# TensorE adds the denominator's two terms in the last five groups of a fused FFT and two-layer MoE kernel

## The chip, the cores and the metric

The kernel runs on one core of one Trainium2 chip. The metric is the device time of one execution in microseconds. Three executions of the kernel before took 1020.41, 1020.96 and 1021.34 us; the median is 1020.96 us.

## The reference

`x` (2 x 3008 x 256, f32) goes through a Fourier transform along the sequence and then along the features, and the real part is kept. The 6016 tokens of 256 features then pass through two dense layers with 2048 hidden units each:

```python
x = fft(fft(x, axis=1), axis=2).real            # 6016 x 256
h = x @ w1_in;  x = (max(h, 0) ** 2) @ w1_out   # first layer
h = x @ w2_in                                   # second layer
P = a[0] + a[1]*h + a[2]*h**2 + a[3]*h**3
Q = 1 + abs(b[0])*abs(h) + abs(b[1])*h**2
out = (P / (Q + 1e-6)) @ w2_out
```

All inputs and outputs are f32.

## The kernel before, in words

Tokens are columns, features and hidden units are partitions. The first layer works on 12 tiles of tokens (one of 384, eleven of 512); the second on 23 sub-tiles, numbered t = 0 to 22: one of 384 tokens and 22 of 256. A sub-tile's 2048 hidden units are 16 chunks of 128. A *group* (t, j) of the second layer is two chunks of 256 tokens side by side, one PSUM bank of 128x512; the last sub-tile, t = 22, has seven such groups (j = 0 to 6) and two single chunks of 128x256 (j = 7 and 8).

Big products are made in parts: each operand is a high and a low part of type F32R, so a chunk costs 3 x 2 matmuls into the hidden layer (line 770) and 3 x 2 out of it (line 824). An F32R matmul is one instruction in the trace. A matmul whose operands are plain F32 is two instructions with two weight loads: the 20 calls of `q_mm` (line 667) have 40 instructions. Both print as f32.

A group of the second layer takes these steps; the letters are the names of the operations in the code:

- `h2` (TensorE, line 770): H2 = W_in x, 12 matmuls of 256 columns for a wide group, 6 for a single.
- `u` (ScalarE, line 890): u = |s h| into SBUF; `t1` (ScalarE, line 904): a3 h + a2.
- `t2`, `t3` (VectorE, lines 920 and 925): Horner's steps for P without a0; both read H2.
- the denominator without its 1, in one of two ways. In most groups `q` (VectorE, line 910) writes (u + b0) h over H2 in the PSUM bank, and `w` (ScalarE, line 916) takes its absolute value in place. In the groups of the list `SUMS`, `v` (ScalarE, line 895) squares a scaled h into SBUF and `w` (GpSimd, line 899) adds it to u. `q` comes after `t3`, since it overwrites H2.
- `y`, `z` (ScalarE, lines 931 and 935): reciprocal square root of the denominator (1 is the bias), then its square, so z = 1/Q. In the groups of the list `ALONE`, `P` (ScalarE, line 939) adds a0 to the polynomial.
- `gh` (VectorE, line 947, or GpSimd, line 946, in `ALONE` groups), `m`, `e` (VectorE, lines 953 and 958 or 962), `c2` (GpSimd, in the last two groups VectorE, line 967): g = P/Q as a high part and a low part that makes up for the rounding.
- `o2` (TensorE, line 824): 12 matmuls (6 for a single) that add the group into the output bank o2a. Of each six, the two with the low part of g come last.

After the 16 chunks of a sub-tile, `oa` (ScalarE, line 984) copies o2a to SBUF, a DMA (line 985) writes it out, and the bank is free for the next sub-tile's first `o2`.

`SUMS` holds the groups of t <= 2 and, in the last two sub-tiles, those with j % 4 == 1. So of the last five groups (22,4) to (22,8), before the change (22,5) is in `SUMS`, (22,4) and (22,6) are in `ALONE`, and (22,7) and (22,8) are the last two (`FIN`).

Every engine executes its instructions in the order of a table: `ORDER` (line 60 on) holds, for each engine, two-digit numbers in base 62, each the place of an operation among those added for that engine. `TIES` holds pairs in which an instruction of GpSimd is made to wait for one of VectorE. `Queues.run` merges the five tables into one program and gives out buffers by an estimate of times; the `cost` given to `add` is such an estimate and has no part in the result. An engine that waits for one instruction's inputs executes nothing that stands behind it in its table.

Of the kernel before, what the change touches and what calls it, by code (L numbers as in the profile page):

```python
# [9 lines left out]
F32 = mybir.dt.float32  # L10
# [39 lines left out]
def f32(ap):  # L50
# [22 lines left out]
    "4w50GWGX4t4x4u4v4yGb4zGdGcGRGi54Ge51GfGS521u53EKGg58GhGk1v55Gn56Gj5759Gp5A5C5BGlGoGmGsGqGu5DGx5GGrGt"
    "5E5FGyGvH2GwGz5H5KH45IH35JH0H1H95OHAH55L5M5P5S5N5QH65RHBHEHF5WHCHD5T5UHJHK5V1wHOHPHG5aHH5X5Y1xHI5ZH7"
    "HLH85bHTHUHM5eHNHQ5cHR5d5i5f5gHSHYHZHV5hHdHW5mHX5jHe5k5lHiHaHjHbHc5n5qHpHf5oHg5p5r5uHqHhHkHl5s5y5tHr"
    "HmHs5vHt5wHuHv5zHzI05x606261HwI4HxI5Hy66I1631y64I265HnI3I66A67I9HoIA68I71z69ELI86EIEIF6BIJIBIKIC6CID"
    "IGIH6D6FIIIO6G6I6HILIMIN6MIP6J6Q6K6LIVIWIaIb6NIQIfIRISIg6R6OIXIY6P6U6SIZ6TIhIcIdIeIkIlIpIqIiIj6V6WIT"
    "6YIUIuImIv6XInIo6Z6cIr6g6a6bIs206dIt6e6fIzIwJ0J4J56hIx6kIy6iJ16jJ26oJ36l6m6n6sJBJC21J6J76p6qJ8JGJH6r"
    "JDJEJF6tJL6w6u70JM6v6xJIJJ6yJKJQ716zJN74JOJR7273J9JV78JWJPJS75JAJT76EMJU79777C7AJaJb7BJXJYJfJg7GJZJc"
    "7KJd7DJe7E7F7H7IJkJlJrJsJh7JJiJj227LJm7M7NJn7OJo7SJtJuJv7P7QJw7RJx7TK17UK2K6K7Jy7VJzK0237WJpK3K4K57X"  # L80
    "7a7YJq7ZKBKC7b7eK87cK9KA7dKDKGKHKLKM7i7fKEKF7gKQKIKJ7hKKKR7mKN7j7kKO7l24KP7nKX257qKYKS7oKT7p7rKU7sKc"
    "7u7tKdKZ7yKaKbKhKi7vKe7wKm7xKnKf827zKgKj8081KkKVKlKrKsKo8384KW86Kp85KwKxKqKtKuKv878826ENL1L2898AL6Ky"
    "Kz8EL08B8CL7L38DL48IL527L8L9LA8FLDLE8G8J8H8KLI8LLJ8MLFLNLOLG8QLHLK8NLL8OLM8P8R8SLB8T8ULP8YLSLTLQLCLR"
    "8VLXLY8W8c8Z8X8aLc8bLULdLV8gLWLZLa28Lb8k8d8eLhLi8h8f8i29Le8jLfLgLjLk8oLlLm8lLn8m8nLtLu8pLyLz8sM3LoM4"
# [1126 lines left out]
```

## Time and profile before

| | |
|---|---|
| median of three executions | 1020.96 us |
| the profiled execution's own time | 1020.44 us |
| its span, first to last instruction | 1018.70 us |
| TensorE busy | 1000.1 us |
| VectorE busy | 977.9 us |
| ScalarE busy | 950.4 us |
| GpSimd busy | 637.3 us |

The profiled execution's time is 1.74 us more than its span: what lies around the first and the last instruction. "Busy" of TensorE counts pipelined matmuls, each printed with its latency (0.28 us for 256 columns) and not with the spacing of a stream (some 0.11 us), so starts, not durations, tell its pace. The clock granted to TensorE is shown as a share of 2.4 GHz.

### The profile page before, as it was taken

The page shows a single profiled execution, that of the slowest core. Times are in us where ns is not written, and L with a number is a line of the kernel's source. Part 1 is how long each engine was busy: PE and PEld are TensorE (multiplying, and loading weights), DVE is VectorE, ACT ScalarE, POOL GpSimd, SP SyncE. Part 2 cuts the span into 40 slices and gives each one's busy share as a digit, 9 for nine tenths or more (in the row PEclk, how much of TensorE's full clock was granted, in tenths as well). Part 3 has the DMA queues.
Part 4 walks back from the last instruction along what each step waited for, and adds up shares of the span by engine and source line. Part 5 has one row for each costly group of instructions (what it writes and reads, how often), then busy time and mean ns, then how long its engine had stood idle before and what let it go on. Part 6 is the DMA issues. An engine that isn't in the chain of part 4 may idle for free.

```text
span 1018.7 us, 20462 instructions
## 1 busy us (share of the span) xinstructions
PE 1000.1 (98%) x7378; PEld 946.5 (93%) x7378; DVE 977.9 (96%) x1766; ACT 950.4 (93%) x1918; POOL 637.3 (63%) x562
## 2 busy tenths in 40 slices
PE   9999999999999999999999999999999999999997
PEld 9989988999999999999999999999999999999986
DVE  5999999898999999999999999999999999999998
ACT  3789998999999999999999999999999999999996
POOL 0000068899866766767676676866766677767486
PEclk9999999999999999999999999999999999999999
DMA  9665500000000000001000001000000000000000
GB/s 346 215 209 160 156 1 1 16 1 27 23 1 17 1 22 12 12 4 30 11 12 11 12 2 32 1 12 22 1 12 26 7 11 12 1 12 9 3 12 22
DMA packets 19701, 38.12 MB, mean 37 GB/s; under 512 B 2078, under 2 KB 12208, under 8 KB 19600
## 3 DMA queue, kind: packets, MB, share of 16 engines
q1 hardware_dynamic: 19487, 36.42, 10.5%
q8 instruction: 58, 0.95, 0.4%
q10 hardware_dynamic: 112, 0.39, 0.1%
q14 instruction: 44, 0.35, 0.1%
HBM read 27.99 MB, written 8.81 MB: 36 GB/s over the span
## 4 chain that ended last, share of the span: by engine, by line
PE 80%; DVE 12%; ACT 3%; DMA 2%; issue 2%; POOL 1%; POOLq 0%; SPq 0%; DVEq 0%; ACTq 0%
PE o2a L824 22%; PE p L770 18%; PE o1a L824 11%; PE o1b L824 11%; PE p L800 9%; PE o2b L770 4%; PE o2b L800 2%; DMA xt<-in_dram 1%; DVE cw L480 1%; DVE g L947 1%; DVE cw L485 1%; DVE t L920 1%; DMA x2l<-in_dram 1%; DVE g L873 1%; PE p L783 1%
## 5 line engine op out<-in xcount | busy, mean ns | idle before, releaser
L824 PE MATMUL o2a<-g,w2hi 128*128 128x256 f32 (+1 forms) x1440 | 256.4, 282 | 4.4 <-POOL g L967 4.0
L873 POOL TENSOR_TENSOR g<-g,g 128x512 fp32r<-128x512 f32 x160 | 208.2, 1304 | 81.6 <-ACT g L867 40.2
L967 POOL TENSOR_TENSOR g<-t,y 128x512 fp32r<-128x512 f32 x150 | 203.2, 1360 | 42.0 <-DVE t L962 20.7
L824 PEld LDWEIGHTS o2a<-g,w2hi 128*128 128x128 f32 x1440 | 207.6, 189 | 9.6 <-POOL g L967 5.5
L848 POOL TENSOR_TENSOR g<-g,bc 128x256 f32<-128x256 f32 x160 | 127.0, 795 | 98.8 <-DVE g L845 39.0
L824 PE MATMUL o2a<-g,w2lo 128*128 128x256 f32 (+1 forms) x720 | 144.2, 280 | 0.0
L824 PE MATMUL o1b<-g,w1hi 128*128 128x512 f32 x352 | 138.3, 393 | 0.0
L824 PE MATMUL o1a<-g,w1hi 128*128 128x512 f32 x352 | 138.2, 393 | 0.0
L899 POOL TENSOR_TENSOR u<-u,y 128x512 f32<-128x512 f32 (+1 forms) x34 | 42.1, 1243 | 140.1 <-ACT y L895 135.6
L770 PE MATMUL p<-x2h,w2hi 128*128 128x256 f32 (+1 forms) x578 | 116.7, 283 | 3.7 <-DVE u L962 2.4
L935 ACT ACTIVATE y<-y 128x512 f32<-128x512 f32 (+2 forms) x187 | 117.7, 630 | 1.8
L770 PE MATMUL p<-x2h,w2lo 128*128 128x256 f32 (+1 forms) x578 | 115.2, 281 | 0.0
L770 PE MATMUL p<-x2l,w2hi 128*128 128x256 f32 (+1 forms) x578 | 115.1, 280 | 0.0
L947 DVE SCALAR_TENSOR_TENSOR g<-t,ab,y 128x512 fp32r<-128x512 f32 (+1 forms) x145 | 110.0, 759 | 3.3 <-ACT y L935 2.2
L863 ACT ACTIVATE g<-g 128x512 fp32r<-128x512 f32 (+1 forms) x172 | 109.3, 635 | 2.8 <-PE o1b L824 0.8
L824 PEld LDWEIGHTS o2a<-g,w2lo 128*128 128x128 f32 x720 | 110.4, 189 | 0.0
L867 ACT ACTIVATE g<-g 128x512 f32<-128x512 f32 (+1 forms) x172 | 108.8, 633 | 1.3
L857 ACT ACTIVATE g<-g 128x512 f32<-128x512 f32 x160 | 102.3, 640 | 3.2 <-POOL g L848 2.7
L920 DVE TENSOR_TENSOR t<-t,p 128x512 f32<-128x512 f32 (+1 forms) x150 | 99.5, 666 | 3.9 <-ACT t L904 3.2
L904 ACT ACTIVATE t<-p,ab 128x512 f32<-128x512 f32 (+1 forms) x150 | 102.4, 685 | 0.0
L770 PEld LDWEIGHTS p<-x2h,w2hi 128*128 128x128 f32 x578 | 90.1, 188 | 9.6 <-DVE u L962 4.4
L890 ACT ACTIVATE u<-p 128x512 f32<-128x512 f32 (+2 forms) x151 | 88.6, 587 | 3.1 <-PE p L770 2.2
(298 smaller groups left out, 2883.4 us busy)
## 6 DMA issues: line engine op xcount, KB each, us to landing
g<-in_dram SPq DMA_DIRECT2D x24, 512.0 KB
xt<-in_dram SPq DMA_DIRECT2D x15, 384.0 KB
out_dram<-os SPq DMA_DIRECT2D x22, 256.0 KB
udram<-U SPq DMA_DIRECT2D x4, 640.0 KB
ut<-udram SPq DMA_DIRECT2D x10, 256.0 KB
x2h<-in_dram SPq DMA_DIRECT2D x4, 512.0 KB
x2l<-in_dram SPq DMA_DIRECT2D x4, 512.0 KB
x<-qdram SPq DMA_DIRECT2D x10, 128.0 KB
```

The lines of the kernel that those rows point to most:

```text
L770: nc.tensor.matmul(h[:, c * n:(c + 1) * n], l[:, k, :], r[:, k], start=(q == 0), stop=(q == 5))
L800: nc.tensor.matmul(h[:, b, c], l[:, b, :], r[:, b, :n], start=(c + q + b == 0), stop=(c == gs - 1 and q == 2 and b == 1))
L824: nc.tensor.matmul(O[t][e], l[:, e * 128:(e + 1) * 128], r[:, c * n:(c + 1) * n], start=(i == 0 and q == 0 and (e == 0 or not one)), stop= ...
L848: return nc.gpsimd.tensor_tensor(out=g[:, 1], in0=g[:, 1], in1=b, op=ALU.subtract)
L863: nc.scalar.activation(out=e["gh"], in_=e["g"], func=ACTF.Square)
L867: nc.scalar.activation(out=e["g"], in_=e["g"], func=ACTF.Square)
L873: return eng.tensor_tensor(out=e["gl"], in0=e["g"], in1=f32(e["gh"]), op=ALU.subtract)
L904: nc.scalar.activation(out=e["t1"], in_=H2[t, j], func=ACTF.Identity, scale=SCALES[0], bias=a2)
L920: nc.vector.tensor_tensor(out=t1, in0=t1, in1=H2[t, j], op=ALU.mult)
L935: nc.scalar.activation(out=z, in_=z, func=ACTF.Square)
L947: return nc.vector.scalar_tensor_tensor(out=e["gh"], in0=e["t3"], scalar=a0, in1=e["z"], op0=ALU.add, op1=ALU.mult)
L967: return (nc.vector if (t, j) in FIN else nc.gpsimd).tensor_tensor(out=e["gl"], in0=e["t1"], in1=e["z"], op=ALU.mult)
```

## The change

The last five groups are put in a list `BY_PE` and taken out of `SUMS`. There, `u` and `v` are made as in `SUMS` groups, and a new operation `pw` on TensorE adds them in PSUM, over H2: a 128x128 unit matrix in plain F32 is the stationary operand, u and v are the moving ones, 512 columns in (22,4), (22,5) and (22,6) and 256 in (22,7) and (22,8). `y` then reads the bank. `q` and `w` of four groups and GpSimd's `w` of (22,5) are gone; the four `w` of ScalarE become four `v`.

```diff
+    BY_PE = [(t, j) for r, (t, j) in enumerate(ROWS2[::-1]) if r < 5]
-    SUMS = [(t, j) for t, j in ROWS2[:-ALONE_END] if t <= 2 or t >= M - 2 and j % 4 == 1]
+    SUMS = [(t, j) for t, j in ROWS2[:-ALONE_END] if (t, j) not in BY_PE and (t <= 2 or t >= M - 2 and j % 4 == 1)]
...
+    def e2_pw(t, j):
+        e = E2[t, j]
+        u, e["w"] = e["w"], H2[t, j]
+        nc.tensor.matmul(e["w"], one_t, u, start=True, stop=False)
+        nc.tensor.matmul(e["w"], one_t, e["z"], start=False, stop=True)
...
+            if key in BY_PE:
+                add(("v",) + key, "ACT", act(n, True), f(e2_v), needs=[("u",) + key], take=(one_of("y", t, j),), after=chained)
+                add(("pw",) + key, "PE", 4 * n * 0.000465 + 0.02, f(e2_pw), needs=[("v",) + key, ("t3",) + key, "one"], after=[("t1",) + key],
+                    give=(free,), lat=0.23)
```

The unit matrix is a new input of 64 KB, loaded by one DMA on SyncE's queue, between the 23rd and the 24th of the 32 weight loads.

All tables are new. They hold the same operations as before but for those named: VectorE has 4 fewer, GpSimd 1 fewer, TensorE 5 more, ScalarE as many. Most places differ by a few: of TensorE's 844 old operations 188 stand elsewhere, none by more than 5 places; of VectorE's 617 of 1731, none by more than 13. SyncE's table differs most (59 of 82, by up to 23 places): among others `qd`, the store of a row that the transform's later tiles need, stands behind 14 weight loads of the first layer where it stood behind 12. The ends of the tables, decoded:

```
TensorE before: h2 22,5 | o2 21,6 | o2 21,7 | h2 22,6 | h2 22,7 | o2 22,0 | h2 22,8 | o2 22,1 | o2 22,2 | ... | o2 22,8
TensorE after:  h2 22,5 | h2 22,6 | o2 21,6 | o2 21,7 | pw 22,4 | h2 22,7 | h2 22,8 | o2 22,0 | pw 22,5 | pw 22,6 |
                o2 22,1 | o2 22,2 | o2 22,3 | pw 22,7 | pw 22,8 | o2 22,4 | ... | o2 22,8

VectorE before: q 22,3 | e 22,0 | m 22,1 | t2 22,4 | e 22,1 | m 22,2 | t3 22,4 | q 22,4 | e 22,2 | t2 22,6 | t2 22,5 | t3 22,6 |
                q 22,6 | m 22,3 | m 22,4 | e 22,3 | e 22,4 | t3 22,5 | t2 22,7 | gh 22,5 | t2 22,8 | m 22,5 | t3 22,7 | e 22,5 |
                q 22,7 | t3 22,8 | m 22,6 | e 22,6 | gh 22,7 | q 22,8 | m 22,7 | e 22,7 | c2 22,7 | gh 22,8 | m 22,8 | e 22,8 | c2 22,8
VectorE after:  q 22,3 | gh 22,1 | m 22,0 | t2 22,4 | e 22,0 | m 22,1 | t3 22,4 | e 22,1 | m 22,2 | t2 22,6 | t2 22,5 | t3 22,6 |
                t3 22,5 | e 22,2 | m 22,3 | m 22,4 | e 22,3 | t2 22,7 | e 22,4 | t2 22,8 | gh 22,5 | m 22,5 | t3 22,7 | t3 22,8 |
                e 22,5 | m 22,6 | e 22,6 | gh 22,7 | m 22,7 | e 22,7 | gh 22,8 | c2 22,7 | m 22,8 | e 22,8 | c2 22,8

ScalarE after:  w 22,3 | u 22,5 | y 22,3 | v 22,4 | u 22,6 | t1 22,5 | t1 22,6 | z 22,3 | P 22,4 | y 22,4 | oa 21 | z 22,4 | v 22,5 |
                u 22,7 | v 22,6 | P 22,6 | t1 22,7 | u 22,8 | t1 22,8 | y 22,5 | z 22,5 | v 22,7 | y 22,6 | v 22,8 | z 22,6 | ... | oa 22
```

## Rows read from the trace of the kernel before

**Rows 1.** Busy time of each engine in stretches, from PE to POOL; then TensorE's granted clock.
```profile
core 0: us, PE busy (x) PEld busy (x) DVE busy (x) ACT busy (x) POOL busy (x), PEclk, DMA share, GB/s
900.00:920.00 20.00, 20.00 (x147) 18.74 (x146) 19.89 (x35) 19.79 (x40) 13.64 (x13) 1.00 0.04 14
960.00:980.00 20.00, 17.03 (x137) 16.04 (x135) 20.00 (x32) 19.03 (x36) 15.51 (x12) 1.00 0.04 15
980.00:990.00 10.00, 9.34 (x79) 9.18 (x78) 10.00 (x17) 10.00 (x20) 8.38 (x8) 1.00 0.01 2
1000.00:1005.00 5.00, 2.72 (x22) 2.36 (x20) 5.00 (x9) 4.91 (x12) 4.57 (x4) 1.00 0.00 2
1005.00:1010.00 5.00, 4.67 (x25) 4.47 (x25) 4.96 (x11) 2.13 (x5) 4.07 (x4) 0.66 0.00 0
```

**Rows 2.** The chain that ended last: start, length, what (its last part).
```profile
998.23 0.74 DVE p L910
1001.42 0.67 DVE o1a L910
...
1008.63 1.27 POOL g L967
1012.16 2.75 PE o2a L824 x20
1014.93 0.60 ACT os L984
```

**Rows 3.** Timeline, VectorE: start, length, line, operation (first to last of the four `q`).
```profile
996.31 0.74 DVE L962 SCALAR_TENSOR_TENSOR u<-p,ab,u 128x512 f32<-128x512 f32 x1
996.98 0.68 DVE L953 SCALAR_TENSOR_TENSOR o2b<-o2b,g 128x512 f32<-128x512 f32 x1
997.57 0.73 DVE L925 SCALAR_TENSOR_TENSOR t<-t,ab,p 128x512 f32<-128x512 f32 x1
998.23 0.74 DVE L910 SCALAR_TENSOR_TENSOR p<-u,ab,p 128x512 f32<-128x512 f32 x1
998.89 0.68 DVE L958 TENSOR_TENSOR t<-t,o2b 128x512 f32<-128x512 f32 x1
...
1001.34 0.75 DVE L910 SCALAR_TENSOR_TENSOR o1a<-u,ab,o1a 128x512 f32<-128x512 f32 x1
1008.12 0.48 DVE L910 SCALAR_TENSOR_TENSOR o1b<-u,ab,o1b 128x256 f32<-128x256 f32 x1
1008.50 0.48 DVE L925 SCALAR_TENSOR_TENSOR x1h<-x1h,ab,p 128x256 f32<-128x256 f32 x1
1010.63 0.48 DVE L910 SCALAR_TENSOR_TENSOR p<-u,ab,p 128x256 f32<-128x256 f32 x1
1011.02 0.42 DVE L953 SCALAR_TENSOR_TENSOR o1b<-o1b,g 128x256 f32<-128x256 f32 x1
```

**Rows 4.** Timeline, TensorE, ScalarE, SyncE: the end; waits in brackets.
```profile
995.01 0.39 PE L770 MATMUL o1a<-x2h,w2hi 128*128 128x256 f32 x2
996.38 0.39 PE L770 MATMUL o1b<-x2h,w2hi 128*128 128x256 f32 x2
1005.28 0.86 PE L824 MATMUL o2a<-g,w2hi 128*128 128x256 f32 x4 [2.56 <-POOL g L967]
1014.39 0.50 PE L824 MATMUL o2a<-g,w2hi 128*128 128x256 f32 x2
1015.55 0.37 SPq L985 DMA_DIRECT2D out_dram<-os  x1
```

**Rows 5.** Busy time as in Rows 1, from the start of `h2 22,7` to TensorE's end.
```profile
996.38:1014.89 18.51, 15.34 (x110) 14.31 (x108) 17.73 (x34) 11.80 (x26) 13.57 (x11) 0.91 0.05 15
```

**Rows 6.** Timeline, TensorE, plain F32 matmuls of the start: 188, 94 and 128 columns.
```profile
12.82 0.51 PE L388 MATMUL p<-c_t,xt 128*128 128x188 f32 x2
13.17 0.58 PE L390 MATMUL p<-c_t,xt 128*128 128x94 f32 x4
13.59 0.51 PE L388 MATMUL p<-c_t,xt 128*128 128x188 f32 x2
...
37.19 2.40 PE L667 MATMUL p<-cd_t,U 128*128 128x128 f32 x20
39.42 0.61 PE L630 MATMUL p<-cd_t,v 128*128 128x128 f32 x4
```

**Rows 7.** Groups of TensorE by shape: count, busy us, mean ns of one (L388 plain F32).
```profile
L388 PE MATMUL o2b<-c_t,xt 128*128 128x188 f32 x12 | 3.1, 338 | 0.0
L824 PE MATMUL o2a<-g,w2lo 128*128 128x384 f32 x16 | 5.4, 337 | 0.0
```

**Rows 8.** Timeline, TensorE, F32R matmuls of 512 columns.
```profile
499.79 0.39 PE L824 MATMUL o1a<-g,w1hi 128*128 128x512 f32 x1
500.02 0.39 PE L824 MATMUL o1b<-g,w1hi 128*128 128x512 f32 x1
```

**Rows 9.** Timeline, ScalarE and GpSimd: `oa 21`, `w 22,4`, `v 22,5`, `w 22,5`.
```profile
995.82 0.59 ACT L984 ACTIVATE os<-o2a 128x512 f32<-128x512 f32 x1
999.05 0.62 ACT L916 ACTIVATE p<-p 128x512 f32<-128x512 f32 x1
999.71 0.60 ACT L931 ACTIVATE g<-p 128x512 f32<-128x512 f32 x1
1000.99 0.60 ACT L895 ACTIVATE g<-p 128x512 f32<-128x512 f32 x1
1002.50 1.27 POOL L899 TENSOR_TENSOR x1l<-x1l,g 128x512 f32<-128x512 f32 x1
```

**Rows 10.** Busy time as in Rows 1, the stretches of the start with TensorE idle.
```profile
0.00:20.00 20.00, 18.65 (x127) 18.07 (x128) 9.53 (x28) 6.65 (x15) 0.20 (x4) 1.00 0.87 327
40.00:60.00 20.00, 18.03 (x141) 17.15 (x140) 19.46 (x51) 16.68 (x43) 0.00 (x0) 1.00 0.17 56
60.00:80.00 20.00, 19.90 (x147) 18.93 (x146) 19.76 (x55) 17.00 (x41) 0.00 (x0) 1.00 0.81 283
140.00:160.00 20.00, 18.54 (x95) 15.83 (x94) 19.34 (x38) 18.57 (x44) 16.29 (x17) 1.00 0.00 1
```

More of the change, by code (lines that the diff above doesn't have):

```diff
@@ new lines @@
+    "0j0k0l0m0n0o12111314160s150t17180u191A1B0v1C1D0w1E1G0x0y1F1I1H0z1J",
+    ACT=
+    "03040G06050J0H0I08070M0L0K00090P0A0N0O0C0S0Q010R0B0V0D0E1a0T1d0U1b0Y0W1e1g0X021c1f0b1h0Z2Q0a2R2T2S2U"
+    "0e2V0c0d1i1j2W0h2X2Y2Z1Y0f0g2a1k2b0k1l0i1Z0j0n2c2d0l0m2f2e2g0F2i2h0q0o0p2l2o0t2j2k2m0r0s2r2n0w2u0u2x"
+    "0v0z2p2q2s0x300y2t12331110362v2w14132y2z391631323C1534353F1817373I1A383A193B3L1C3O3D1m3G1B3E3H1D1E1G"
+    "3R3U3J3K3M1F3N3X1I1H3a3P1K3S3Q3T1J3d1M3g3V1L3W3Y1n1O3Z3j1N3m3b1Q3c3e1P3f1S3p3s3h1o3i1R3k1p3l1U3v1T3n"
@@ new lines @@
+    "DeS6SESFDdS7S8DfDiSJSBSCRxSKDgSDDhDjSGRySHDmDkSOSISPDlSLDnSMDoDpDqDuSNSQSRSSSTSUDvDrDsSYDySZDtDwDxSf"
+    "SVSWSgE2SXDzSaE0SbE1E3E6ScShSiSkSjSlE4E5E7EASpSqE8E9SmEBSnEESoSrSsStSuSvEFECSdSzT0EDEGSeEHT4T5T9TASw"
+    "SxT1SyETT2T6T3TBTETFT7TLTMTRTCTSTDT8TGTHTITNTWTQTOTXTTTPTcTUTiTdTbTYTjTVTZThTaToTeTtTfTpTuTgTJTkTzTK"
+    "TlTqTmU0TnTrTvTsU7TwU8U4UDUETyUIU1UJU2TxU3UCUOU9UPUAUFUBUNUKUGUUUVULUHUMUTUQUaURUWUfUbUgUSUZUXU5U6UY"
+    "UcUlUhUkUmUqUrUdUeUnUiUsUjUoUpUtUuUvUw",
+    DVE=
+    "0O0P0Q010R020S0T030W0U050X040Y0Z0V060a070b090e0f080c0g0d0h0A0m0i0n0B0o0D0C0j0E0k0p0l0q0H0r0u0I0s0v0t"
@@ new lines @@
+    "QiQdQoQRQpQtQeQnQfQbQgQcQuQsR3QlQhR4QqR2QmQrR8QxR9QvQyQwR7QzRDR0RERCRNR1R5RORMRSRARTR6RHRBRIRRRJRFRW"
+    "RGRKRXRLRPRfRaRgRbRQRURYRVRjRZRpRcRdRkRqReRhRiRlRmRnRrRoRsRtRu",
+    PE=
+    "0001040203050607080A090B0C0F0G0D0E0J0H0I0K0Q0S0R0T0L0U0M0N0V1C1E0W1G1D0O1I1F0X1H0P1J1K1M1O1Q1S1U1L1N"
+    "1W1Y1a1P1R1c1e1g1T1V1i1X1k1Z1m1b1o1d1q0Y1f1h1s1u0Z1j1l1w1y1n1p20221r1t24261v1x282A1z0a210b2C23252E27"
+    "7O292G7Q2B2D2I7S7U2F7W2H7P7Y7R7a2J7T7c7V7e0c7X7g0d7Z7b7i7k7d2K7m7f2M7o7h2O7j7q2L2Q7s2N7u0e7l7n2S2P7p"
@@ L171 @@
+    "8u8r8t8v8x8w8y",
 )
 TIES = (
[L175 to L179 removed]
@@ L278, in body @@
 def body(ctx: ExitStack, tc: tile.TileContext, x0, xf, w1, w2, a_in, b_in,
-         w0i, c47, cd, r0, out):
+         w0i, c47, cd, r0, one, out):
     nc = tc.nc
@@ L295, in body @@
     ab = const.tile([128, 8], F32, name="ab")
+    one_t = const.tile([128, 128], F32, name="one_t")
     beta = const.tile([128, NF], F32, name="beta")
@@ L333, in body @@
         add(("const", 2 + i), "SP", 0.8, lambda o=o, a=a: nc.sync.dma_start(out=o, in_=a), lat=4.0)
+    add("one", "SP", 0.8, lambda: nc.sync.dma_start(out=one_t, in_=one), lat=3.0)
     add("abs", "ACT", 0.1, lambda: nc.scalar.activation(out=ab[:, 4:6], in_=ab[:, 4:6], func=ACTF.Abs),
@@ L435, in body @@
         for dc in range(2):
-            add(("um", c, dc), "PE", (0.383 * n + 0.06 * (n == 1)) if c else 0.9, lambda c=c, dc=dc, g=tags[dc]: u_mm(c, dc, g),
+            add(("um", c, dc), "PE", (0.4 * n + 0.06 * (n == 1)) if c else 0.9, lambda c=c, dc=dc, g=tags[dc]: u_mm(c, dc, g),
                 needs=[("x", c)] + ([("hot", c)] if c and HOT[c - 1] and not dc else []), take=(tags[dc],), give=("xt",) if dc else (), lat=0.2)
@@ L889, in e2_u @@
         e["w"] = sb(tag2("u", t, j), [128, NMAX])[:, :e["n"]]
-        nc.scalar.activation(out=e["w"], in_=H2[t, j], func=ACTF.Abs, scale=SCALES[2 if (t, j) in SUMS else 1])
+        nc.scalar.activation(out=e["w"], in_=H2[t, j], func=ACTF.Abs, scale=SCALES[2 if (t, j) in SUMS + BY_PE else 1])
     def e2_v(t, j):
@@ L928, in e2_y @@
         e = E2[t, j]
-        if (t, j) not in SUMS:
+        if (t, j) not in SUMS + BY_PE:
             e["z"] = sb(tag2("y", t, j), [128, NMAX])[:, :e["n"]]
@@ L998, in chain @@
             return []
-        return [("v" if op == "y" and order[key] in SUMS else op,) + order[key]]
+        return [("v" if op == "y" and order[key] in SUMS + BY_PE else op,) + order[key]]
     for t, j in ORDER1:
@@ L1064, in body @@
                 after=[("v",) + key] if sums else [], give=((held,) if alone else (half,)) if sums else ())
-            add(("y",) + key, "ACT", act(n, not sums), f(e2_y), needs=[("w",) + key],
-                take=() if sums else (one_of("y", t, j),), after=[] if sums else chained)
+            add(("y",) + key, "ACT", act(n, not sums), f(e2_y),
+                needs=[("pw" if key in BY_PE else "w",) + key],
+                take=() if sums or key in BY_PE else (one_of("y", t, j),), after=[] if sums or key in BY_PE else chained)
             add(("z",) + key, "ACT", act(n), f(e2_z), needs=[("y",) + key])
```

209 lines of the change are left out of this document (96 added, 113 removed).

## The prediction

> **What bounds the kernel now.** I read the busy times by stretch first. Up to 960 us TensorE is the bound: 20.00 of 20 us, with VectorE just behind it at 19.89 [rows 1]. From 960 us on the roles change: VectorE has no gap (20.00 of 20, then 10.00 of 10 and 5.00 of 5) while TensorE waits, 2.97 us before 980, 0.66 before 990, 2.28 after 1000, and then runs a stretch with a mean granted clock of 0.66, that is, in part at the lower of its two levels [rows 1]. The chain that ended last confirms it: it runs through VectorE, two of the four `q` lie on it, and near the end it passes to GpSimd, to 2.75 us of TensorE, to the copy and the store [rows 2]. From TensorE's last matmul, which ends at 1014.89, to the end of the span are 3.81 us; the change leaves these alone.
>
> **What the change removes.** VectorE loses four `q`. By start to start they take 0.66 us each for the wide ones (998.23 to 998.89; the one at 1001.34 is alike) and 0.38 and 0.39 us for the singles (1008.12 to 1008.50, 1010.63 to 1011.02) [rows 3]: 2.09 us. All of it is on VectorE's unbroken line, so VectorE alone would end 2.1 us sooner. GpSimd loses its addition of (22,5), 1.27 us [rows 9]. ScalarE gains and loses nothing: a `w` takes 0.62 us and the `v` that stands in for it 0.60 [rows 9].
>
> **What it adds: the price of `pw`.** Each of the five is two plain F32 matmuls, so four instructions in the trace. No row has 512 columns of plain F32; the nearest is the transform's with 188. Two such instructions take 0.35 us from start to start (12.82 to 13.17), 0.175 each [rows 6]. The narrow ones say less: 94 columns take 0.105 (0.42 for four) and 128 columns 0.11 (2.23 for twenty) [rows 6], so below 128 something other than the columns sets the spacing. The row that decides is a duration: an instruction with 188 columns of plain F32 takes 338 ns, one with 384 columns of F32R 337 [rows 7]. A plain F32 instruction thus holds the array as long as an F32R one with twice its columns. F32R with 512 columns is spaced 0.23 us [rows 8], so I take 0.46 for a plain one: 1.84 us for a wide `pw`, 0.92 for a single, 3 x 1.84 + 2 x 0.92 = 7.36 us in all. The bounds: if at 512 columns plain F32 streamed like F32R, 4 x 0.23 = 0.92 and 3.68 in all; if the slope between the 128 and the 188 row held (0.0635 us for 60 columns), 0.52 each, 2.07 and 8.3 in all. I take the middle one because it is nearest to the 188 row, which scaled by columns gives 0.477. The estimate written into the diff, 0.97 us for 512 columns, stands for both matmuls of the group; the 188 row scaled gives that for one.
>
> **Where it lands.** Follow TensorE from 996.38, the start of `h2 22,7`, to its end at 1014.89: 18.51 us [rows 4, 5]. Twelve F32R matmuls take 1.37 us there (995.01 to 996.38) [rows 4]. What remains is one such dozen for the two `h2` singles, seven for `o2 22,0` to `o2 22,6` and one for the two last `o2`: 9 x 1.37 = 12.33 us. The other 6.18 us are slack: waits, the longest 2.56 us [rows 4], and matmuls at the lower clock (mean 0.91 [rows 5]). Into 6.18 us of slack go 7.36 us of `pw`. So TensorE takes the end over from VectorE, and the slack can't even be used in full, since the first `pw` waits.
>
> That wait: `pw 22,4` stands before the two last `h2` and needs `t3 22,4`. Before, that step ran from 997.57 to 998.23. In the new table `m 22,2` and `e 22,1` stand behind it, 0.59 and 0.67 us [rows 3], so it ends at 996.97; with some 0.2 us for the wake-up `pw 22,4` starts at 997.15. TensorE has all that stands before it in both tables done at 996.38, so 0.77 us are lost. Queued behind the waiting `pw` are the last two `h2`, for which ScalarE's `u 22,7` and `u 22,8` wait, and `o2 22,0`. From 997.15 on TensorE has 12.33 + 7.36 = 19.69 us of work and ends at 1016.84, 1.95 us later than before, if nothing else holds it. Little else should: `o2 22,0` needs the bank that ScalarE's `oa 21` frees, which now stands behind `y 22,4` and so behind the first `pw`. With `pw` done at 998.99, `y` and `oa` of 0.6 us each free the bank at about 1000.4, when TensorE, done with the two `h2`, is just ready for it. The last groups arrive in time: before, 3.37 us lie between the end of `q 22,8` (1011.02) and TensorE's last pair (1014.39) [rows 3, 4], a `w` among them; with `pw 22,8` done near 1011.4 the low part of (22,8) is there near 1014.8, before TensorE asks for it at 1016.6. VectorE's 2.1 us become waiting time.
>
> **The rest.** The 64 KB of the unit matrix cost under 0.3 us of transfer (283 GB/s in the stretch from 60 to 80 us [rows 10]) and go out among weight loads long before the last groups; I cost them at nothing. If that cover were gone, the first `h2` groups would wait for the weights by these 0.3 us. New tables cannot make TensorE faster where it is at 20.00 of 20; they can move its idle time at the start, 1.35 us before 20, 1.97 between 40 and 60, 1.46 between 140 and 160 [rows 10], and that between 960 and 996. `qd`, later on SyncE's queue, is needed from the third tile on alone. I take 0, with 1 us either way.
>
> **Sum.** The profiled execution: 1018.70 span + 1.74 around it = 1020.44; plus 1.95 makes 1022.4. The median of the three executions lies 0.5 us above that one, so I forecast 1022.9 us for a median, slower by 0.19%. The likeliest case's own range is 1021.5 (no wait at `pw 22,4`, a price at the 128 row's spacing scaled, 0.446) to 1024.5 (the 188 row scaled, half a microsecond of further waits, 1 us from the tables).
>
> **Rivals.**
> *Plain F32 streams wide columns at full pace.* Then `pw` costs 3.68 us in all, it fits into the slack, and TensorE ends at 997.15 + 12.33 + 3.68 = 1013.16: 1.7 us sooner, 1018.7 by the profiled execution and 1019.2 as a median. VectorE's saved 2.1 us allow it. This one ends on the other side; it decides by the spacing of one `pw` instruction with 512 columns, and the balance is at 0.34 us (4 x 1.36 = 5.44 = 1014.89 - 997.15 - 12.33 with five `pw` worth four wide ones). For it: the narrow rows hardly grow with the columns. Against it: 338 against 337 ns [rows 7]. In the Trainium skill, "TensorE: Matmul & The Clock Gate", section "Back-to-back issue gap", gives N/2.4 + 2.5 ns for a matmul of N columns without naming a type for it: 0.216 us at 512 columns, by which a wide `pw` of four would be 0.86 us and this rival would hold; for the 188 columns it gives 0.081 us, and the trace shows 0.175. Where they differ I follow the trace. Chance 0.17.
>
> *The wait at the first `pw` grows.* `t3 22,4` or `v 22,4` comes late, since `gh 22,1` and `m 22,0` now stand ahead of `t2 22,4` on VectorE and wait for ScalarE, and `v 22,4` has `w 22,3`, `u 22,5` and `y 22,3` ahead of it. Each microsecond there is one at the end, since TensorE has no slack behind it, and `oa 21`, behind `y 22,4`, passes it on to `o2 22,0`. Three steps of 0.66 us late are 2 us: 1024.9. For it: ScalarE is at 10.00 of 10 there [rows 1]. Against it: both tables have the same work ahead of these steps but for the two moved behind. Chance 0.13.
>
> *The new tables give the time back.* TensorE's waits from 960 to 990, 3.6 us [rows 1], or at the start shrink by 2 us or so, and the end comes out at 1021. Against it: between 960 and 996 VectorE has no gap to close and the same work to do. Chance 0.10.
>
> **How the numbers follow.** The likeliest case has 0.60. About 0.2%, 2.0 us, is what a measurement of this kernel tells from no change; measured against 1020.96 that puts the borders at 1018.9 and 1023.0. The forecast lies close to the upper one: of its 0.60, 0.30 go to slower and 0.30 to same. The first rival lies close to the lower one: 0.09 faster, 0.08 same. The second is slower, 0.13; the third same, 0.10. Together: faster 0.09, same 0.48, slower 0.43. The range runs from 1018.8, inside the first rival, to 1025.0, just past the second's centre.
>
> **What would show it.** In the profile after: matmuls into p, o1a and o1b banks with the unit matrix, four per group, spaced 0.46 us (0.23 for singles); a wide `pw` near 1.84 us. TensorE with hardly a wait from `pw 22,4` to its end and no stretch below a granted clock of 1.00 in the last 20 us; the chain that ended last on TensorE for its last 15 us or more, VectorE and ScalarE waiting for `pw` and with gaps. A spacing of 0.23 us, or VectorE still without a gap up to the end, would prove the forecast wrong; so would a TensorE wait of over 2 us before the first `pw`, or an end that moves while the last 60 us do not.

## The result, and the profile after

The changed kernel takes 1027.08 us (median of six executions, 1026.21 to 1027.56) against 1020.89 us for the kernel before (also six): ratio 1.0061, 95% interval 1.0048 to 1.0074. It is 6.2 us slower. The forecast was 1022.9 us with a range up to 1025.0, so the sign and part of the mechanism were right and the size was not.

| | before | after |
|---|---|---|
| span of the profiled execution, us | 1018.7 | 1025.6 |
| TensorE busy, us | 1000.1 | 1006.4 |
| VectorE busy, us | 977.9 | 979.7 |
| ScalarE busy, us | 950.4 | 951.4 |
| GpSimd busy, us | 637.3 | 634.8 |

The stretches of [rows 1], after; columns from PE to POOL are busy us and counts, then TensorE's granted clock:

```profile
900.00:920.00 20.00, 20.00 (x152) 18.99 (x151) 19.48 (x35) 19.71 (x40) 13.25 (x13) 1.00 0.05 15
960.00:980.00 20.00, 16.21 (x136) 15.50 (x135) 20.00 (x33) 19.23 (x37) 10.77 (x10) 1.00 0.04 15
1000.00:1005.00 5.00, 4.82 (x31) 3.66 (x30) 4.78 (x8) 4.57 (x10) 3.85 (x3) 1.00 0.01 3
1005.00:1010.00 5.00, 4.86 (x23) 2.96 (x21) 4.13 (x8) 4.49 (x11) 3.49 (x3) 1.00 0.14 52
```

After 1000 us TensorE is nearly full and VectorE and ScalarE have the gaps; before it was the other way round. The clock stays at 1.00 where the kernel before had a stretch at 0.66. The chain that ended last (start, length, what), after, against [rows 2]:

```profile
1001.01 0.67 DVE t L934
1001.68 0.04 issue
1001.72 1.12 PE p L903 x2
1002.85 0.87 PE p L904 x2
...
1006.67 1.12 PE p L903 x2
1007.80 0.86 PE p L904 x2
1008.66 0.86 PE o1a L903 x2
1009.51 0.86 PE o1a L904 x2
1010.37 4.25 PE o2a L827 x36
1014.62 0.43 PE o1b L903 x2
...
1016.35 5.54 PE o2a L827 x48
1021.88 0.02 issue
1021.91 0.60 ACT os L993
```

From 1006.67 us to the copy of the output the chain is TensorE without a break, and the `pw` (lines 903 and 904) lie on it. The timeline, after, shows who waits for them, against [rows 3, 4]:

```profile
1000.94 0.73 DVE L934 SCALAR_TENSOR_TENSOR t<-t,ab,p 128x512 f32<-128x512 f32 x1
1001.72 1.12 PE L903 MATMUL p<-x1l,one_t 128*128 128x512 f32 x2 [0.18 <-DVE t L934]
...
1015.52 0.38 ACT L940 ACTIVATE y<-o1b 128x256 f32<-128x256 f32 x1 [3.72 <-PE o1b L904]
1016.39 0.48 DVE L956 SCALAR_TENSOR_TENSOR g<-x1h,ab,y 128x256 fp32r<-128x256 f32 x1 [1.55 <-ACT y L944]
```

So far this is what was foretold for the end. But `t3 22,4` runs at 1000.94 and not at 996.31 (997.57 less the two steps moved behind it [rows 3]): it is 4.6 us late before any `pw` has run. In what follows, *lateness* is the start of a step of VectorE, ScalarE or GpSimd less the start of the same step in the kernel before, from the two traces, as the median of all steps in a stretch. Each row is one profiled execution (us; the head is the time in the kernel before at which a stretch of 10 to 40 us begins; the names are those of the experiments below):

```
                               40   200   240   440   500   550   560   600   680   900   980
after                        1.92  1.53  2.23  2.04  2.48  2.54  3.58  3.31  3.33  4.56  4.63
e1_new_tables_old_end        1.18  0.78  1.81  1.57  2.01  2.07  3.09  2.82  2.96  3.11  3.17
e2_old_tables_new_end        0.07  0.29  0.28  0.04  0.04  0.04  0.03  0.03  0.03  0.08  0.38
e3_new_start                 1.29  0.89  0.87  0.57  0.57  0.56  0.57  0.57  0.57  0.58  0.71
e9_order_200_950             0.12  0.04  1.08  0.91  1.32  1.39  2.43  2.22  2.53  2.72  2.78
e10_order_500_660_timed      0.23  0.27  0.25  0.31  0.57  0.93  1.97  1.70  2.92  2.91  2.89
e14_order_500_660_one_tie    0.13 -0.02 -0.04 -0.46 -0.08  0.29  0.37  0.32  1.28  1.27  1.29
e15_after_one_tie            1.27  0.82  1.51  1.31  1.75  1.62  1.70  1.66  1.97  2.17  2.22
```

Of the 6.9 us of span, 4.6 us are there before the end begins; 2.3 us come from the end. The lateness falls by some tenths in places, but most of what is lost at 40 us or at 560 us arrives at 1020 us.

### The profile page after: what moved, and what is told of

It is laid out like the page before. It is cut to its first block, busy times and chain, and to the rows that moved or that the text cites. A ratio compares the mean times of both kernels' runs of the same rounds, so it can differ in the third digit from the quotient of the medians.

```text
span 1025.6 us, 20505 instructions
## 1 busy us (share of the span) xinstructions
PE 1006.4 (98%) x7398; PEld 949.3 (93%) x7398; DVE 979.7 (96%) x1762; ACT 951.4 (93%) x1918; POOL 634.8 (62%) x561
## 4 chain that ended last, share of the span: by engine, by line
PE 83%; DVE 9%; ACT 4%; issue 2%; DMA 1%; POOL 0%; SPq 0%; DVEq 0%; POOLq 0%
PE o2a L827 22%; PE p L773 18%; PE o1a L827 11%; PE o1b L827 11%; PE p L803 8%; PE o2b L773 4%; PE o2b L803 2%; PE p L786 2%; PE p L788 2%; PE o2b L827 1%; DVE g L956 1%; DMA x2h<-in_dram 1%; DVE t L929 1%; PE p L633 1%; DVE t L934 1%
## 5 line engine op out<-in xcount | busy, mean ns | idle before, releaser
L851 POOL TENSOR_TENSOR g<-g,bc 128x256 f32<-128x256 f32 x160 | 124.7, 780 | 109.8 <-DVE g L848 48.7
L956 DVE SCALAR_TENSOR_TENSOR g<-t,ab,y 128x512 fp32r<-128x512 f32 x144 | 111.8, 777 | 3.5 <-ACT y L944 1.9
L929 DVE TENSOR_TENSOR t<-t,p 128x512 f32<-128x512 f32 (+1 forms) x153 | 101.6, 665 | 3.6 <-ACT t L913 1.7
L913 ACT ACTIVATE t<-p,ab 128x512 f32<-128x512 f32 (+1 forms) x153 | 104.5, 687 | 0.0
L893 ACT ACTIVATE u<-p 128x512 f32<-128x512 f32 (+1 forms) x151 | 89.2, 592 | 6.0 <-PE p L773 5.3
```

What stands on the lines that cost most here:

```text
L851: return nc.gpsimd.tensor_tensor(out=g[:, 1], in0=g[:, 1], in1=b, op=ALU.subtract)
L913: nc.scalar.activation(out=e["t1"], in_=H2[t, j], func=ACTF.Identity, scale=SCALES[0], bias=a2)
L929: nc.vector.tensor_tensor(out=t1, in0=t1, in1=H2[t, j], op=ALU.mult)
L956: return nc.vector.scalar_tensor_tensor(out=e["gh"], in0=e["t3"], scalar=a0, in1=e["z"], op0=ALU.add, op1=ALU.mult)
```

## The experiments

Where only `ORDER` differs, operations and results are the same. Kernels with an old end have `BY_PE = []` and load the unit matrix without using it. `TIES`, as pairs of operations, are the same 172 in the kernels before and after; the two kernels with a newly ordered end below have 168, since four pairs of the last two sub-tiles are gone. A new order also makes `Queues.run` give out the PSUM banks of `h1` and `h2` anew, up to the kernel's end. That alone costs nothing to be seen: with the order of 500 to 660 us changed, 121 of the 127 such results behind 680 us lie in another bank than before, and the lateness stays at 2.9 us from there to 980 us. A cost in us is the ratio less 1, times 1020.

**Which half costs it?**

*New tables up to about 950 us, old ones from there:*

```diff
-    BY_PE = [(t, j) for r, (t, j) in enumerate(ROWS2[::-1]) if r < 5]
+    BY_PE = []
```

> The tables of after up to about 950 us, the tables of before from there on, and no group in BY_PE: VectorE, GpSimd and ScalarE make every denominator as before; the unit matrix is loaded and not used. Theory (most of the loss lies upstream, in the new order of the work before 950 us, where steps of the kernel after are 1.9 us late at 120 us and 4.6 us late at 950 us): 1025.0 to 1026.0 us, 4 to 5 above before. Rival (the loss is made by the five pw at the end, and the lateness upstream would be made up there): 1020.5 to 1021.5, as before.

1023.37 us, ratio 1.0033 (1.0022 to 1.0043): 3.4 us for tables alone, where no operation is added but the load of the unit matrix. The rival is refuted; the theory wanted more.

*Old tables up to about 950 us, the changed end (`BY_PE` as in the change):*

> The tables of before up to about 950 us, those of after from there on, with the five pw. Theory (upstream order): 1022.5 to 1023.5 us, some 2 above before, as the prediction had it from the price of pw. Rival (the end makes the loss): 1026 to 1027.5, as after.

1022.72 us, ratio 1.0027 (1.0016 to 1.0039): as the theory said. Its chain is the changed kernel's, 4.24 us sooner (`pw 22,4` at 997.48). The two halves, 0.0033 and 0.0027, make 0.0060 of 0.0061.

**Is it the price of `pw` at the end?** As the last, with the operands of `pw` in F32R, the unit matrix rounded once by ScalarE:

```diff
+        if (t, j) in BY_PE:
+            e["w"] = e["w"].bitcast(F32R)
...
-        nc.tensor.matmul(e["w"], one_t, u, start=True, stop=False)
+        nc.tensor.matmul(e["w"], one_r, u, start=True, stop=False)
```

> As the run with the old tables and the new end, but the operands of pw are F32R (u, v and the unit matrix are rounded to it), so each matmul of pw is one instruction and not two, expected at 0.23 us for 512 columns; the denominators of the five groups are less exact. Theory (at the end TensorE is the bound by the price of pw, 6.9 us): the price falls to about 1.7 us, TensorE fits and VectorE's saved 2.1 us show: 1018.7 to 1020.2 us. Rival (the end loses by the wait of pw for t3 and v and by what is queued behind it, not by the price): 1022 to 1023, hardly below the run without F32R.

1019.67 us, ratio 0.9992 (0.9982 to 1.0001): as the theory said, 0.0035 below the kernel with plain F32. A `pw` matmul of 512 columns now starts every 0.23 us (its timeline, TensorE):

```profile
1002.73 0.39 PE L909 MATMUL p<-g,one_r 128*128 128x512 f32 x1
1002.96 0.39 PE L908 MATMUL o1a<-u,one_r 128*128 128x512 f32 x1
1003.18 0.39 PE L909 MATMUL o1a<-y,one_r 128*128 128x512 f32 x1
```

VectorE's saved 2.1 us are not gained in full, since the end then hangs on GpSimd (its chain):

```profile
1007.78 1.31 POOL g L961
1009.09 1.26 POOL g L982
...
1010.98 1.35 POOLq L1227
1012.33 0.04 issue
1012.37 2.63 PE o2a L828 x20
```

**Where in the tables?** With the old end and new order in one stretch only. *Up to 200 us:*

> The tables of after up to about 200 us (the transform's start, the weight loads, the first two tiles), the tables of before from there on, no group in BY_PE. Theory (upstream order): 1022.3 to 1023.0 us, the 1.5 to 1.9 us by which the kernel after is late at 200 us carried to the end, since TensorE has no idle time behind it to make it up. Rival 1 (the end makes the loss): 1020.5 to 1021.5. Rival 2 (all the lateness grows from the start): 1025 or more.

1021.17 us, ratio 1.0009 (0.9999 to 1.0018). Less than expected; by its time alone not told from nothing. Its lateness at 40 us is 1.29, though, and 0.9 to 1.9 in all five profiles with the new start, against -0.1 to 0.4 in the others.

*From 200 to 400 us, one execution:*

> The tables of before, but for the stretch from about 200 to 400 us, which has the order of after; no group in BY_PE. Read by lateness: the time of each step of VectorE, ScalarE and GpSimd less its time in the kernel before, median of 40 us. Theory (single waits that the new order makes are never made up, since TensorE is the bound): 0.7 to 1.0 us late from 240 us on, where the kernel after shows TensorE waiting 0.6 us for VectorE, and as late at 950 us; 1021 to 1022 us. Rival (lateness of the middle is noise of an execution, or caught up by the old order): under 0.3 us late at 950 us.

1021.87 us; lateness -0.1 at 200, 0.58 at 240, 0.93 at 440 and the same at 900, as the theory had it. *From 500 to 660 us, one execution:*

> The tables of before, but for the stretch from about 500 to 660 us, which has the order of after; no group in BY_PE. Theory (waits that the new order makes are never made up): about 1 us late from 560 to 580 us on, and as late at 950 us. Rival (noise, or caught up): under 0.3 us late at 950 us.

1023.01 us; lateness 0.39 at 440, 0.98 at 550, 2.02 at 560, 2.60 from 680 on: more than expected. Under the old order single executions differ by up to a microsecond too (below), so this kernel was run eleven times, and the whole middle beside it. *From 200 to 950 us:*

> Order of the kernel after from 200 us to 950 us, of the one before ahead of it and behind it; no pw; nothing left out. Theory (the new order delays TensorE at several places between 200 and 950 us, nothing takes it up again): the whole order up to 950 us cost 3.3 us and that up to 200 us 0.9 us, so 2.4 us remain: ratio 1.0018 to 1.0030. Rival (the 3.3 us come from the start, and the middle is innocent; the lateness seen there in single looks is that of the execution): within 0.0008 of 1.

1023.18 us, ratio 1.0027 (1.0018 to 1.0036), as the theory had it. *From 500 to 660 us again:*

> The kernel of the look at 500 to 660 us once more, now timed. Theory (the new order costs something in this stretch alone): the look had it 2.2 us later from there, of which some 0.5 can be that execution's own, so 1.0 to 2.2 us: ratio 1.0010 to 1.0022. Rival (what that look showed was the execution): within 0.0008 of 1.

1023.21 us, ratio 1.0023 (1.0014 to 1.0032): 160 us of reordered work cost 2.3 us where the whole middle costs 2.8; in the table above 1.0 us falls between 550 and 560 us. But some 0.7 us belong to the place near 660 us where the new order meets the old one. There TensorE waits for a `c2` of GpSimd, and its own lateness goes from 2.2 to 2.9 us; its timeline in this kernel:

```profile
661.53 0.74 PE L827 MATMUL o2a<-g,w2hi 128*128 128x256 f32 x4 [0.37 <-POOL g L976]
```

The kernel with the whole middle changed has no such wait there. Its lateness grows by 1.6 us from 440 to 680 us (0.91 to 2.53), so this stretch holds rather more than half of what the middle costs.

**By what?** There one VectorE step takes 1.89 us in place of 0.75. The timelines of VectorE (`gh 10,4`) and GpSimd (`c2 10,3`), before:

```profile
556.91 0.75 DVE L947 SCALAR_TENSOR_TENSOR g<-t,ab,y 128x512 fp32r<-128x512 f32 x1
557.13 1.70 POOL L967 TENSOR_TENSOR g<-t,y 128x512 fp32r<-128x512 f32 x1 [0.68 <-DVE t L962]
```

after:

```profile
558.43 0.74 DVE L971 SCALAR_TENSOR_TENSOR t<-t,ab,o2b 128x512 f32<-128x512 f32 x1
559.29 1.89 DVE L956 SCALAR_TENSOR_TENSOR g<-t,ab,y 128x512 fp32r<-128x512 f32 x1
559.32 1.32 POOL L976 TENSOR_TENSOR g<-t,y 128x512 fp32r<-128x512 f32 x1 [0.70 <-DVE t L971]
```

Before, `gh` came 0.22 us ahead of `c2`, ran at its own 0.75, and `c2` was held (1.70 in place of 1.32). After, `gh` starts 0.86 us behind `e 10,3` where it started 0.66 behind it (its `z 10,4` ends at 559.26, 558.63 + 0.63 on ScalarE; before, at 556.72, it was in time). So both start within 0.03 us, and now `gh` is held for 1.14 us. It is 1.88 to 1.90 in all five profiles with the new order and without a tie there. I therefore made `c2 10,3` wait for `gh 10,4`, and, against a second hold (`gh 13,0`, 1.38), `c1 8,3` for `gh 13,0` (it was tied to an earlier step of VectorE, `gh 12,7`):

```diff
-    "...8xRj8zRq"
+    "...8xRj8zRq4YFi5VIM"
```

> As the timed order of 500 to 660 us, with two ties more: GpSimd's c2 10,3 waits for VectorE's gh 10,4, and c1 8,3 for gh 13,0. Nothing left out. Theory (the new order costs its time there because those two gh start beside a GpSimd operation and are held up by it, 1.89 and 1.38 us in place of 0.75): both are back at 0.75, the step of about 1.0 us at 560 us and that of 0.8 near 650 are gone, ratio 1.0002 to 1.0012 where it was 1.0023. Rival (the long gh are a sign and not the cause; TensorE loses its time to the order of its own queue): the steps stay, ratio 1.0018 or more.

1023.06 us, ratio 1.0026 (1.0015 to 1.0036): no gain, as the rival had it. But the step at 560 is gone (lateness 0.44 at 550, 0.51 at 560), and a new one is there at 680 (2.36). The second tie is at fault; the timeline of GpSimd and TensorE in this kernel:

```profile
656.47 1.30 POOL L876 TENSOR_TENSOR g<-g,g 128x512 fp32r<-128x512 f32 x1 [3.49 <-DVE g L956]
661.05 0.73 PE L827 MATMUL o2a<-g,w2hi 128*128 128x256 f32 x4 [1.32 <-POOL g L976]
```

GpSimd stands still for 3.49 us for `gh 13,0`, and TensorE later waits 1.32 us for GpSimd. The first tie by itself, `"...8zRq4YFi"`:

> The timed order of 500 to 660 us with one tie more: GpSimd's c2 10,3 waits for VectorE's gh 10,4. Without the second tie, which held c1 8,3 back by 3.5 us and took away again what the first had given. Nothing left out. Theory (the hold of 1.14 us at gh 10,4 is the cause of the step at 560 us, and TensorE loses by it what VectorE does): ratio 1.0008 to 1.0016 where it was 1.0023 without the tie. Rival (the step comes back later in the stretch in any case): 1.0020 or more.

1021.98 us, ratio 1.0014 (1.0005 to 1.0023), as the theory had it and 0.0009 below the kernel without the tie. The two intervals overlap, but the traces are plain: lateness goes from 0.29 at 550 to 0.37 at 560 where it went from 0.93 to 1.97, and TensorE's own matmuls fall 0.03 us further behind from 560 to 575 us (0.32 to 0.35) where they fell 0.97 (0.78 to 1.75). `gh` is back at 0.75 (timeline of VectorE and GpSimd):

```profile
557.22 0.75 DVE L956 SCALAR_TENSOR_TENSOR g<-t,ab,y 128x512 fp32r<-128x512 f32 x1
558.06 1.31 POOL L976 TENSOR_TENSOR g<-t,y 128x512 fp32r<-128x512 f32 x1 [1.52 <-DVE g L956]
```

In the changed kernel, with three ties (`4YFi5VIM1H6x`; the third, `c2 1,7` after `m 2,0`, is told of below) and with the first alone:

> The changed kernel with three ties more: GpSimd's c2 10,3 after VectorE's gh 10,4, c1 8,3 after gh 13,0, c2 1,7 after m 2,0. Nothing left out. Theory (VectorE held up by GpSimd in the new order is part of what the tables cost): 1.0 to 2.0 us less than the 1027.1 of the changed kernel, ratio 1.0042 to 1.0052; the rest is the start and the end. Rival (the holds are made up elsewhere): 1.0058 or more.

> The changed kernel with that one tie and nothing else. Nothing left out. Theory: 0.8 to 1.4 us less than the 1027.1 of the changed kernel, ratio 1.0046 to 1.0053. Rival: within 0.4 us of it, 1.0057 or more.

1025.55 us, ratio 1.0051 (1.0038 to 1.0065), and 1025.12 us, ratio 1.0045 (1.0031 to 1.0059), against 1.0061: the first as its theory had it, the second a shade lower. With four characters in `TIES` the median is 1.6 us lower; the intervals overlap. The traces give the tie 1.0 us of it: lateness goes from 1.62 to 1.70 from 550 to 560, where the changed kernel's goes from 2.54 to 3.58.

**A version that beats both?** *Plain F32 for two groups only, (22,4) and (22,6), the end reordered, old tables up to 950 us:*

```diff
+    BY_PE = [(22, j) for j in [4, 6]]
```

> The tables of before up to about 950 us; only (22,4) and (22,6) are added by TensorE, in plain F32, and the end of the tables is ordered anew with pw counted at the 1.72 us that it takes. Theory (the price decides: 3.4 us of pw fit into TensorE's slack of 6.2 us at the end, and VectorE is rid of 1.3 us): 0.5 to 1.3 us under before, a ratio of 0.9987 to 0.9995. Rival (pw's waits in TensorE's queue cost more than VectorE gains, whatever the price): at or above before, 1.000 to 1.002.

1021.23 us, ratio 1.0003 (0.9994 to 1.0012): no gain, as the rival had it. *Five groups in F32R, the end reordered for its price:*

> The tables of before up to about 950 us, all five groups by TensorE with F32R operands, and the end of the tables ordered anew with a wide pw counted at the 0.46 us that it takes. Theory (the price decides): with 1.7 us of pw VectorE's saved 2.1 us show in full or nearly: 1.3 to 2.1 us under before, a ratio of 0.9979 to 0.9987, the fastest of all. Rival (the end's chain through GpSimd and VectorE leaves no more than the 0.5 us of the earlier F32R run): 0.9992 to 1.000.

1020.92 us, ratio 1.0003 (0.9994 to 1.0012): no gain, just above the rival's 0.9992 to 1.000. Both profiles show `m 2,0` at 231 us held by GpSimd's `c2 1,7` for 1.3 us, under the very order that leaves it alone in other kernels. The second kernel's timeline:

```profile
231.69 2.26 DVE L968 SCALAR_TENSOR_TENSOR u<-u,g 128x512 f32<-128x512 f32 x1
232.06 1.34 POOL L982 TENSOR_TENSOR g<-u,y 128x512 fp32r<-128x512 f32 x1
```

and that of the first F32R kernel:

```profile
231.13 0.98 DVE L968 SCALAR_TENSOR_TENSOR u<-u,g 128x512 f32<-128x512 f32 x1
231.52 1.77 POOL L982 TENSOR_TENSOR g<-u,y 128x512 fp32r<-128x512 f32 x1
```

`m` took 0.96 to 0.99 us in eleven profiles and 2.26 or 2.27 in four. The lateness does not follow it alone: at 440 us it is 0.04 in the kernel with two groups and 1.03 in the other, of which 0.77 was there at 200 us already. A tie for it, in the first F32R kernel:

> The kernel with the matmuls of pw in F32R and the old order up to 950 us, and one tie more: GpSimd's c2 1,7 waits for VectorE's m 2,0, which in some profiles took 0.98 us and in others 2.27 (then GpSimd's 1.77 or 1.33), under the same order. The sum in the five groups is less exact. Theory (which engine goes first there is decided anew in every execution, and costs some 0.7 us where it is GpSimd): m takes 0.98 always, the times spread less, and the median is 0 to 0.5 us lower, ratio 0.9985 to 0.9993. Rival (the tie costs GpSimd as much as it gives VectorE): 0.9996 or more.

1019.79 us, ratio 0.9996 (0.9986 to 1.0005), against 1019.67 without the tie: no gain, as the rival had it, and the executions spread no less (1018.9 to 1022.3; 1018.9 to 1020.5 without). So which engine wins there is not what spreads them. No kernel is shown to beat the one before.

## Why the prediction failed, by its steps

**The step that failed** is "The rest": "New tables cannot make TensorE faster where it is at 20.00 of 20", and "I take 0, with 1 us either way." They cost 3.4 us with the old end (2.2 to 4.4), and 4.6 us in the profile of the changed kernel; with 3.4 in the place of 0 the sum gives 1026.3 us. I had bounded the term by TensorE's visible idle time, and asked only whether the tables could give time back. That they could make TensorE slower where it showed no idle time was not considered.

What stood there in its place, as far as it was followed: `gh 10,4` meets `c2 10,3`, and VectorE loses 1.14 us. What it makes next comes late, and TensorE, in order, pauses three times between 567 and 575 us, each time at a matmul that waits for a step of VectorE: 0.24, 0.31 and 0.34 us. The kernel before and the one with the stretch from 500 to 660 us and one tie have none of these pauses. The one of 0.31 us is for x2l, the low part of the second layer's input, which VectorE makes in two steps. The timeline of VectorE (second step of x2l) and TensorE, before:

```profile
564.84 0.68 DVE L883 TENSOR_TENSOR x2l<-o1b,x2h 128x512 fp32r<-128x512 f32 x1
566.22 0.39 PE L770 MATMUL p<-x2l,w2hi 128*128 128x256 f32 x2
566.44 0.39 PE L770 MATMUL p<-x2h,w2hi 128*128 128x256 f32 x2
```

and after:

```profile
568.42 0.68 DVE L886 TENSOR_TENSOR x2l<-o1b,x2h 128x512 fp32r<-128x512 f32 x1
568.85 0.70 PE L773 MATMUL p<-x2l,w2hi 128*128 128x256 f32 x2
569.39 0.40 PE L773 MATMUL p<-x2h,w2hi 128*128 128x256 f32 x2
```

Before, x2l was done at 565.52, 0.70 us ahead of the pair of matmuls that reads it. After, it is done at 569.10, when the pair has begun: its second matmul starts at 569.16, 0.31 us behind the first, and the next pair starts 0.54 us after this one in place of 0.22. No waits are listed for TensorE there, since a matmul's printed 0.28 us cover nearly all of the 0.31. The stretch as busy time, before and after:

```profile
560.00:580.00 20.00, 20.00 (x160) 19.26 (x159) 19.96 (x35) 19.80 (x41) 13.16 (x13) 1.00 0.01 2
```

```profile
560.00:580.00 20.00, 19.90 (x150) 18.41 (x149) 19.93 (x34) 18.82 (x39) 12.23 (x12) 1.00 0.00 1
```

TensorE is "busy" 20.00 and 19.90 us, 0.10 apart; the weight loads, the second column, are 0.85 us apart, and 10 matmuls fewer are done. The Trainium skill says so in "Perfetto Trace Analysis", section "Identifying the Most-Contended Engine": busy time of matmuls is a poor measure because they are pipelined, and the load of weights a better one. The trace agrees, and my 20.00 of 20 [rows 1] was the poor one.

The traces show a second part that needs no wait: TensorE's pace. Two F32R matmuls of 256 columns in a row start 0.113 us apart, or some 0.118 for a stretch of five to over a hundred of them, at a granted clock of 1.00 either way. Six matmuls from start to start, in the changed kernel and in the one with a single tie more (timelines of TensorE):

```profile
886.18 0.63 PE L827 MATMUL o2a<-g,w2hi 128*128 128x256 f32 x4
886.89 0.64 PE L827 MATMUL o2a<-g,w2hi 128*128 128x256 f32 x4
```

```profile
884.22 0.62 PE L827 MATMUL o2a<-g,w2hi 128*128 128x256 f32 x4
884.89 0.62 PE L827 MATMUL o2a<-g,w2hi 128*128 128x256 f32 x4
```

They take 0.71 and 0.67 us. From 850 to 900 us the changed kernel's profile has the slow pace in most places, which costs it 0.8 to 1.0 us more than the other profiles, four of which run the same order there; with this its lateness comes to 4.56 at 900 us. Over 200 to 950 us, what two matmuls of one operation take beyond 0.1135 us from start to start (0.2275 at 512 columns), pauses left out, comes to 4.9 to 5.6 us in the five profiles with the whole new order there, and to 4.0 to 4.6 us in the seven with the old. So about 1 us of the middle's cost goes with the pace. What sets it no run shows.

Shown by experiment: that the order alone costs 3.4 us, that rather more than half of the middle's share lies between 500 and 660 us, and that the hold at `gh 10,4` is worth about 1 us. Not shown: why the new order has more of the slow pace, the rest of that stretch (`gh 13,0` at 1.37 us remains with the first tie; the tie against it made a worse wait), and which entries of the new start cost its 0.9 us.

**The price of `pw`:** right, a little high. In the chain above the second wide one ends at 1008.66 and the third at 1010.37: 1.72 us for four instructions, 0.43 each, and a single is 0.86 (1014.62 to 1015.48). In all 3 x 1.72 + 2 x 0.86 = 6.88 us for 7.36. That 188 columns of plain F32 take as long as 384 of F32R [rows 7] carried over: 0.43 against 0.23 at 512 columns. The rival in which plain F32 streams at the pace of F32R is out. The formula of the Trainium skill beside it ("TensorE: Matmul & The Clock Gate", section "Back-to-back issue gap") gives 0.216 us for 512 columns without naming a type, as the gap of an isolated matmul; that is near the F32R kernel's 0.23 and half of this one's 0.43.

**Where it lands:** right in kind, 0.8 us short in size. TensorE takes over the end, and `pw 22,4` waits for `t3 22,4` as foretold: 997.15 plus the 4.6 us inherited is 1001.75. From the start of `t3 22,4` to that of `pw` I had 0.84 us, with 0.2 for the wake-up, for which no row of before stood; it is 0.78 (1000.94 to 1001.72). I put the end at +1.95 us; alone it measured 2.8 (1.6 to 4.1). Its profile shows the difference: `pw 22,4` starts at 997.48 in place of 997.15, since VectorE's new end is 0.38 us late there, and from then to TensorE's end it is 20.16 us in place of 19.69 (20.15 in the changed kernel). `pw` is 0.5 us cheaper in that sum and the rest 0.9 us dearer; 0.3 of this is a wait before the second `pw` for `t3 22,5`, where I had written that little else should hold TensorE. With "The rest" at nothing, as in the kernel with the old tables, the ratio 1.0027 makes 1023.7 us of the 1020.89: 0.8 us above the forecast and inside its range.

**VectorE's 2.1 us become waiting:** right (1.55 and 3.72 us of waits in the timeline above), and the unit matrix's load costs nothing to be seen: 0.05 and 0.07 us of lateness at 40 us in the first two kernels with the old start and a new end.

**What would show it wrong:** "an end that moves while the last 60 us do not" was on record and is what came in half: before the last 60 us lie 4.6 of 6.9 us by the two profiles, and 3.4 of 6.2 by the two halves run apart.

## What to carry to other kernels

When a change comes with a new instruction order, the order is an edit of its own: price it, and if it can't be priced, give it a range with a tail towards slower: here a new order lost 3.4 us, mostly where the engine that bounds the kernel showed no idle time. To see a loss on a pipelined engine, compare starts of the same step in both traces, or weight loads, not busy time. Before blaming the new operation, run its half and the order's half apart: two kernels settled that here.

## What the runs showed of the hardware

- VectorE and GpSimd hold each other up for whole instructions: `gh` (inputs t and y in SBUF) 0.75 or 1.89 us, `c2` 1.70 or 1.32. In the traces of all kernels, when a `c2` starts 0.1 to 0.3 us after a `gh`, GpSimd is held, all of some 200 times (sub-tiles 3 to 20); at 0.03 us or less VectorE is, five of five times, although its record starts first. It is not so for every pair: `m 2,0` starts 0.4 us ahead of `c2 1,7`, and either was held. In the Trainium skill, "SBUF — State Buffer", section "Who interferes with whom", an instruction of VectorE with two inputs in SBUF contends with one of GpSimd that reads SBUF, and whoever issues first blocks the other in full. The trace agrees on the blocking; by the recorded starts the order of the two does not decide a dead heat.
- A shift of 0.2 us in when a step becomes ready (`gh 10,4`) turned a hold of 0.38 us on an engine with time to spare into one of 1.14 us on one without.
- Plain F32 through a unit matrix costs 0.43 us per instruction of 512 columns, two instructions per matmul; F32R 0.23, one instruction.
- F32R matmuls of 256 columns follow each other at 0.113 us or at some 0.118, for a stretch, at a granted clock of 1.00. Over 200 to 950 us that makes up to 0.6 or 0.7 us between two profiles of one order.
